# V's products in one run over all queries, the memory's normaliser applied to phi, and buffers kept as rings

## The chip, the cores and the metric

The kernel runs on one core of a Trainium2 chip. A core has TensorE (PE in the rows; its weight loads are PEld), VectorE (DVE), ScalarE (ACT), GpSimd (POOL) and SyncE, whose queue (SP) issues all the DMAs of this kernel. TensorE writes to PSUM, 8 banks of 512 fp32 columns in each of 128 partitions; the other data lie in SBUF. The metric is the device time of one execution in microseconds (us), less being better.

## The reference

Four batches, 8 heads, 576 queries of 64 elements: causal attention plus a linear "memory", mixed by a gate per head. The result is a 2304 x 512 matrix that goes through two feed-forward layers.

```
scores = scale * q @ k.T ; causal mask ; a = softmax(scores) ; local = a @ v
q_p  = where(q > 0, q, exp(q) - 1) + 1                    # phi(q)
mem_ret  = einsum('bhsd,bhde->bhse', q_p, M_prev)
mem_norm = einsum('bhsd,bhd->bhs', q_p, z_prev)[..., None] + 1e-06
g = 1 / (1 + exp(-beta))
x = g * mem_ret / mem_norm + (1 - g) * local              # to (2304, 512)
h = x @ w_in ;  x = (h * cos(h)) @ w_out                  # layer 1, inner width 2048
h = x @ w_in2 ; out = (h * tanh(softplus(h))) @ w_out2    # layer 2
```

## The kernel before, in words

Heads are worked on in pairs: 16 pairs (4 batches of 4), a pair being 128 partitions (two heads of 64). Queries come in 5 blocks of a pair, four of 128 and a last one of 64, in which the two heads stand side by side. The attention is a generator of 80 steps, one for each pair and block i, written as a pipeline: in step s, stage_c works on step s-4, then stage_b on s-2, then stage_a on s. prep of the next pair is called where i is 3.

- prep loads k, q, the memory's matrix, v and q once more, and makes phi (`ph`, transposed: 128 head elements x 576 queries) with two ScalarE instructions and one of VectorE (L217 to L219).
- stage_a: the scores on TensorE (L238, for the last block L251), masked minimum on VectorE (L240), exponential on ScalarE (L243), reciprocal of the sum (L263), and a scaling by it and by 1 - g on GpSimd (L265). Where i is 0 it calls memory first.
- memory multiplies each block of phi (as the weights) with the memory's matrix and the two normalisers beside it, 130 columns (L277), divides on VectorE (L280 to L282), and leaves `mo`, the memory's part by queries.
- stage_b transposes the scaled exponentials on TensorE (L297, L303); ScalarE or VectorE copies them to `aT` (L115, L117, the helper scaled).
- stage_c, for each block i: `mo` is transposed into a PSUM tile `o` by a product with the identity (L313), V's products add to it, for each of the i + 1 blocks of keys and each head one of 64 weight columns (L324); ScalarE makes the high part `xH` (L328) and VectorE the low part `xL` (L329), which are stored once per pair (L331, L332).

A product of two fp32 operands shows as two MATMUL records of one form in the trace, a transpose as one. The feed-forward layers split each operand in a high and a low fp32r part and use three products (L420 for h, L478 and L487 for y). Layer 1 is woven into the attention from batch 1 on (`next(m1)` in the main loop, paced by the steps of stage_c), and so is the conversion of its weights (L119 to L133, L163). What is left of layer 1, and all of layer 2, comes after the attention. A scheduler orders each engine's instructions when the program is built, from its own model of their times; on the chip each engine runs its list in that order, with semaphores between engines. A tile with `bufs=N` has at most N copies alive; which memory they have is found at that time too.

Of the kernel before, what the change touches and what calls it, by code (L numbers as in the profile page):

```python
# [20 lines left out]
BUFS = dict(  # L21
    mb=2, kd=4, qd=4, aD=4, vt=2, qt=1, ph=2, den=2, mo=4, xH=1, xL=3, sm=7, mn=2, at=8, aT=7, u=2, e=3, g=4, h=4, y=4, xb=3, yp=3, yh=2, yl=2, wst=2, S=6, T=8,
)
# [7 lines left out]
LAGC = 4  # L31
# [4 lines left out]
    wh="ap", aT="av", yl="p", ml="vp", y0="v", y1="a", aD="v",  # L36
# [7 lines left out]
def attention_moe_moe_kernel(  # L44
# [4 lines left out]
    qp: bass.AP,  # L49
    vn: bass.AP,  # L50
    mbd: bass.AP,
    beta: bass.AP,
# [51 lines left out]
    counts = {}  # L104

# [72 lines left out]
    def attention(ap, pools):  # L178
# [14 lines left out]
        def bank(tag, shape, name):  # L193
            turn[tag] += 1
            return pools[0].tile(shape, F32, tag=tag, name=name, bufs=BUFS[tag])

        pairs = [(b, p) for b in range(B) for p in range(NP)]
        prepd = {}

        def prep(b, p):  # L200
            st = {}

            kd = ap.tile([P, S], F32, tag="kd", name="kd", bufs=BUFS["kd"])
            nc.sync.dma_start(kd, kT[b, p])
            qd = ap.tile([P, S + D], F32, tag="qd", name="qd", bufs=BUFS["qd"])
            nc.sync.dma_start(qd, qT[b, p])
            st["q"], st["k"] = qd, kd
            mz = ap.tile([P, P + 2], F32, tag="mb", name="mz", bufs=BUFS["mb"])
            nc.sync.dma_start(mz, mbd[b, p])
            st["mz"] = mz  # L210
            vt = ap.tile([P, NQ, P], F32, tag="vt", name="vt", bufs=BUFS["vt"])
# [7 lines left out]
            nc.vector.scalar_tensor_tensor(ph, qt, 0.0, ph, ALU.max, ALU.add)  # L219
            st["ph"] = ph  # L220
            st["xH"] = ap.tile([P, S], F32R, tag="xH", name="xH", bufs=BUFS["xH"])
            st["xL"] = ap.tile([P, S], F32R, tag="xL", name="xL", bufs=BUFS["xL"])
            prepd[b, p] = st

        def stage_a(b, p, i):
# [6 lines left out]
            ats = [ap.tile([P, S], F32, tag="at", name="at", bufs=BUFS["at"]) for _ in range(2 if i < 4 else 1)]  # L232
# [35 lines left out]
        def memory(b, p):  # L268

            st = prepd[b, p]  # L270
            out = ap.tile([P, NQ, P], F32, tag="mo", name="mo", bufs=BUFS["mo"])
            for c0, c1 in ((0, 3), (3, NQ)):
                nb = c1 - c0
                mp = bank("T", [P, nb, P + 2], "mp")
                for c in range(c0, c1):
                    q0 = min(c * P, S - P)
                    nc.tensor.matmul(mp[:, c - c0], st["ph"][:, q0:q0 + P], st["mz"], start=True, stop=True)  # L277
                den = ap.tile([P, nb, 2], F32, tag="den", name="den", bufs=BUFS["den"])
                gg = igate[:, 2 * p:2 * p + 2].rearrange("q (o h) -> q o h", o=1).broadcast_to([P, nb, 2])
                nc.vector.scalar_tensor_tensor(den, mp[:, :, P:], 1e-6, gg, ALU.add, ALU.mult)  # L280
                nc.vector.reciprocal(den, den)  # L281
                nc.vector.tensor_tensor(  # L282
                    out[:, c0:c1].rearrange("q c (h d) -> q c h d", h=2),
                    mp[:, :, :P].rearrange("q c (h d) -> q c h d", h=2),
                    den.rearrange("q c (h o) -> q c h o", o=1).broadcast_to([P, nb, 2, D]), ALU.mult)
            st["mo"] = out

        def stage_b(b, p, i):
            st = prepd[b, p]
            n = P if i < 4 else D  # L290
            aTs = []
            for at in st["at", i]:
                tp = bank("T", [P, SM], "tp")
                aT = ap.tile([P, SM], F32, tag="aT", name="aT", bufs=BUFS["aT"])
                W = P * min(i + 1, 4)
                for c in range(0, W, P):
                    nc.tensor.transpose(tp[:, c:c + P], at[:, c:c + P], ident)  # L297
                scaled("aT", aT[:, :W], tp[:, :W], first=b == 0)
                aTs.append(aT)
            if i == 4:  # L300
                aD = ap.tile([P, 2, D], F32, tag="aD", name="aD", bufs=BUFS["aD"])
                tp = bank("T", [P, SM], "td")
                nc.tensor.transpose(tp[:D, :P], at[:, SM:], ident)  # L303
                scaled("aD", aD.rearrange("p a b -> p (a b)")[:D, :P], tp[:D, :P])
                aTs.append(aD)
            st["aT", i] = aTs

        def stage_c(b, p, i):
            st = prepd[b, p]
            n = P if i < 4 else D  # L310
            q0 = i * P
            o = bank("T", [P, P], "o")
            nc.tensor.matmul(o[:, :n], st["mo"][:, i], ident[:, P - n:], start=True, stop=False,  # L313
                             skip_group_check=True)
            for c in range(i + 1):
                kk = P if c < 4 else D
                for j in range(2):
                    if i < 4:
                        a = st["aT", i][j][:, c * P:(c + 1) * P]
                    elif c < 4:  # L320
                        a = st["aT", i][0][:, c * P + j * D:c * P + (j + 1) * D]
                    else:
                        a = st["aT", i][1][:D, j]
                    marks["pe"] = nc.tensor.matmul(  # L324
                        o[j * D:(j + 1) * D, :n], st["vt"][:kk, c, j * D:(j + 1) * D], a,
                        start=False, stop=c == i, skip_group_check=True).ins
            xH = st["xH"]
            nc.scalar.activation(xH[:, q0:q0 + n], o[:, :n], AF.Copy)  # L328
            nc.vector.tensor_tensor(st["xL"][:, q0:q0 + n], o[:, :n], xH[:, q0:q0 + n].bitcast(F32), ALU.subtract)  # L329
            if i == 4:  # L330
                nc.sync.dma_start(xsH[p, :, b * S:(b + 1) * S], xH.bitcast(F32))  # L331
                marks["sp"] = nc.sync.dma_start(xsL[p, :, b * S:(b + 1) * S], st["xL"].bitcast(F32)).ins  # L332
                del prepd[b, p]
# [333 lines left out]
```

## Time and profile before

| what | value |
|---|---|
| median of 3 runs | 1071.06 us (1069.19 to 1071.45) |
| profiled execution, first to last instruction | 1068.0 us |
| TensorE busy in it | 1042.6 us, 98% |
| VectorE, ScalarE, GpSimd busy | 490.7, 485.8, 391.6 us |

The profiled execution is given as its span; the times of the runs also hold what lies before the first and after the last instruction, some 3 us. "Busy" counts the time in which at least one record of an engine is open. Records of TensorE overlap, since products are pipelined, so the distance between starts tells more than the length of a record.

### The profile page before, as it was taken

To read this page: it belongs to the slowest core of one execution; us is meant where nothing else is said; L and a number is where in the kernel's file an instruction comes from. 1 tells how busy PE (TensorE), PEld (TensorE's weight loads), DVE (VectorE), ACT (ScalarE), POOL (GpSimd) and SP (SyncE) were. 2 spreads that over 40 slices of the span, in tenths; PEclk is the share of its full clock that TensorE was granted. 3 is DMA by queue.
4 is the path that set the end of the run, shared out by engine and by line. 5 is a ranking of instruction groups with operands and counts; after the bars stand their busy time and mean duration, and the time that the engine had idled before them with its cause. 6 is when DMAs were issued, how large, how long until landed. Compare 5 with 4: busy or idle time off the path is not lost.

```text
span 1068.0 us, 17139 instructions
## 1 busy us (share of the span) xinstructions
PE 1042.6 (98%) x6512; PEld 873.7 (82%) x6512; DVE 490.7 (46%) x1136; ACT 485.8 (45%) x1023; POOL 391.6 (37%) x425
## 2 busy tenths in 40 slices
PE   6997999999999999999999999999999999999998
PEld 4666688787878899998888889888888888888897
DVE  4588885445554558776766655665000000000000
ACT  6797875556564534344535454543322321222131
POOL 3377853323232334555555555654101010110100
PEclk8999999999999999999999999999999999999999
DMA  6366642323121275425345355630300300110010
GB/s 235 119 196 224 205 135 82 119 83 122 59 87 46 73 266 190 139 90 198 110 166 177 111 176 185 228 119 22 116 1 1 118 1 0 60 40 1 21 41 20
DMA packets 66369, 116.99 MB, mean 110 GB/s; under 512 B 5616, under 2 KB 25072, under 8 KB 66288
## 3 DMA queue, kind: packets, MB, share of 16 engines
q1 hardware_dynamic: 66288, 115.91, 32.2%
q8 instruction: 51, 0.84, 0.3%
q14 instruction: 30, 0.25, 0.1%
HBM read 87.58 MB, written 28.31 MB: 109 GB/s over the span
## 4 chain that ended last, share of the span: by engine, by line
PE 92%; ACT 2%; DVE 2%; DMA 2%; issue 1%; POOL 1%; SPq 0%; DVEq 0%; POOLq 0%; ACTq 0%
PE h L420 37%; PE y L478 20%; PE y L487 18%; PE o L324 5%; PE sp L238 4%; PE tp L297 4%; PE o L313 2%; PE mp L277 1%; PE sp L251 1%; DMA qt<-in_qp_dram 1%; DMA wst<-in_w1i_dram 1%; DVE at L240 1%; ACT at L243 1%; DMA vt<-in_vn_dram 1%; POOL at L265 0%
## 5 line engine op out<-in xcount | busy, mean ns | idle before, releaser
L420 PE MATMUL h<-xbH,w 128*128 128x256 f32 (+1 forms) x1536 | 393.0, 338 | 0.1
L420 PEld LDWEIGHTS h<-xbH,w 128*128 128x128 f32 x1536 | 266.9, 190 | 33.7 <-issue 1.0
L420 PE MATMUL h<-xbL,w 128*128 128x256 f32 (+1 forms) x768 | 258.0, 336 | 1.5 <-DMA xbL<-xsL 1.5
L478 PE MATMUL y<-g,w 128*128 128x256 f32 (+1 forms) x1344 | 221.5, 319 | 4.4 <-ACT aT L115 4.2
L478 PEld LDWEIGHTS y<-g,w 128*128 128x128 f32 x1344 | 193.1, 192 | 30.8 <-issue 9.4
L487 PE MATMUL y<-w,g 128*128 128x512 f32 x864 | 201.8, 389 | 0.0
L487 PEld LDWEIGHTS y<-w,g 128*128 128x128 f32 x864 | 161.9, 188 | 33.5
L392 DVE TENSOR_TENSOR g<-e,g 128x512 fp32r<-128x512 f32 x36 | 24.9, 691 | 297.1 <-ACT g L115 297.1
L420 PEld LDWEIGHTS h<-xbL,w 128*128 128x128 f32 x768 | 145.6, 190 | 16.9 <-DMA xbL<-xsL 1.7
L392 POOL TENSOR_TENSOR g<-e,g 128x512 fp32r<-128x512 f32 x36 | 47.8, 1328 | 286.5 <-ACT g L115 286.5
L265 POOL TENSOR_SCALAR at<-at,sm,omg 128x128 f32<-128x128 f32 (+2 forms) x144 | 102.7, 723 | 134.4 <-DVE sm L263 119.2
L384 ACT ACTIVATE e<-h 128x512 f32<-128x512 f32 x72 | 43.0, 597 | 232.5 <-PE h L420 231.0
L392 POOL TENSOR_TENSOR g<-u,g 128x512 fp32r<-128x512 f32 x72 | 102.0, 1436 | 121.5 <-ACT g L115 45.6
L367 ACT ACTIVATE u<-h 128x512 int32<-128x512 f32 x72 | 42.9, 595 | 111.9 <-PE h L420 104.2
L243 ACT ACTIVATE at<-at,mn 128x128 f32<-128x128 f32 (+3 forms) x128 | 70.9, 555 | 28.2 <-DVE mn L240 26.8
L129 DVE SCALAR_TENSOR_TENSOR wst<-wst 128x512 int32<-128x512 int32 x64 | 53.9, 843 | 37.7 <-POOL wst L119 31.3
L119 POOL TENSOR_SCALAR wst<-wst 128x512 f32<-128x512 f32 x64 | 46.4, 731 | 63.2 <-DMA wst<-in_w1i_dram 25.1
L297 PE MATMUL tp<-ident,at 128*128 128x128 f32 x384 | 63.9, 285 | 5.6 <-DVE den L281 2.2
L368 DVE SCALAR_TENSOR_TENSOR u<-u,h 128x512 f32<-128x512 int32 x72 | 49.0, 682 | 40.8 <-ACT u L367 40.5
L240 DVE CUSTOM_DVE_ANT_0 at<-sp,mask 128x128 f32<-128x128 f32 (+3 forms) x128 | 59.3, 482 | 17.6 <-PE sp L238 16.0
L133 DVE TENSOR_TENSOR wst<-wst 128x512 int32<-128x512 int32 x64 | 66.1, 1035 | 1.2
L324 PE MATMUL o<-aT,vt 128*64 128x128 f32 (+1 forms) x896 | 64.5, 272 | 1.7 <-ACT aT L115 1.5
(76 smaller groups left out, 1084.1 us busy)
## 6 DMA issues: line engine op xcount, KB each, us to landing
wst<-in_w1i_dram SPq DMA_DIRECT2D x16, 512.0 KB, 5.4
wst<-in_w1o_dram SPq DMA_DIRECT2D x16, 512.0 KB, 4.6
wst<-in_w2i_dram SPq DMA_DIRECT2D x16, 512.0 KB, 4.0
wst<-in_w2o_dram SPq DMA_DIRECT2D x16, 512.0 KB, 4.7
qd<-in_qT_dram SPq DMA_DIRECT2D x16, 320.0 KB, 3.4
vt<-in_vn_dram SPq DMA_DIRECT2D x16, 320.0 KB, 3.2
xbH<-xsH SPq DMA_DIRECT2D x20, 256.0 KB, 4.9
xbL<-xsL SPq DMA_DIRECT2D x20, 256.0 KB, 4.6
```

Source lines behind the costliest of these rows:

```text
L129: nc.vector.scalar_tensor_tensor(lo, hi, 3, lo, ALU.logical_shift_left, ALU.bitwise_or)
L133: nc.vector.tensor_tensor(dst, lo, hi, ALU.bitwise_xor)
L240: nc.vector.tensor_tensor_reduce(at[:, :N], sp[:, :N], mask[:, SM - q0:SM - q0 + N], SSC, 3.0e38, ALU.add, ALU.min, mn[:, j:j + 1])
L243: marks["act"] = nc.scalar.activation(at[:, :N], at[:, :N], AF.Exp, bias=mn[:, j:j + 1], scale=-1.0, accum_out=sm[:, j:j + 1]).ins
L265: turn_of("sc", b == 0).tensor_scalar(at[:, :N], at[:, :N], sm[:, j:j + 1], gates[j], ALU.mult, ALU.mult)
L297: nc.tensor.transpose(tp[:, c:c + P], at[:, c:c + P], ident)
L324: marks["pe"] = nc.tensor.matmul(o[j * D:(j + 1) * D, :n], st["vt"][:kk, c, j * D:(j + 1) * D], a, start=False, stop=c == i, skip_group_ch ...
L368: nc.vector.scalar_tensor_tensor(u, u.bitcast(I32), -TWO_PI, h, ALU.mult, ALU.add)
L392: turn_of(kind).tensor_tensor(gL, g, gH.bitcast(F32), ALU.subtract)
L420: nc.tensor.matmul(h[:, a * T:(a + 1) * T], w_[:, c, f0:f0 + P], x_[c], start=m == 0, stop=m == 3 * NC - 1)
L478: nc.tensor.matmul(y[e // per][:, cols], w_[:, f, es], g_, start=fst and m == 0 and e % per == 0, stop=lst and m == 2, skip_group_check=True)
L487: nc.tensor.matmul(y[t], g_[:, tsl], w_[:, f, :], start=fst and m == 0, stop=lst and m == 2, skip_group_check=True)
```

## The change

V's products of a pair wait until all its 5 blocks have been transposed, and run over all queries at once: for each block of keys and head, one product over all queries from that block on (512, 448, 320, 192 and 64 columns) into one bank `o`, and two small ones for the first 64 queries into another, `od`. The memory's normaliser is applied to phi, which is now laid out by queries: GpSimd multiplies phi with z, VectorE sums and takes the reciprocal, GpSimd scales phi; TensorE transposes the result (`pT`, copied by ScalarE), and the memory's matrix is multiplied once with all queries, straight into `od` and `o`. `mo`, its identity product and its division go. xH and xL are made in two instructions each per pair instead of five. Many tiles become slices of one larger tile used in turn (ring), kd and qd with 2 places instead of 4, xL with 2 instead of 3; `aT` is one tile for two pairs. On the host, q is laid out by queries (640 with padding) and z is handed over as rows, broadcast over partitions by a DMA of its own.

```diff
+    def ring(pool, tag, shape, dtype=F32):
+        if tag not in rings:
+            rings[tag] = [pool.tile([shape[0], BUFS[tag], *shape[1:]], dtype, name=tag), 0]
+        r = rings[tag]
+        r[1] += 1
+        return r[0][:, (r[1] - 1) % BUFS[tag]]
...
         def prep(b, p):
...
-            qt = ap.tile([P, S], F32, tag="qt", name="qt", bufs=BUFS["qt"])
-            nc.sync.dma_start(qt, qp[b, p])
-            ph = ap.tile([P, S], F32, tag="ph", name="ph", bufs=BUFS["ph"])
+            qt = ring(ap, "qt", [P, NQ, P], F32)
+            nc.sync.dma_start(qt, qn[b, p])
+            ph = ring(ap, "ph", [P, NQ, P], F32)
             nc.scalar.activation(ph, qt, AF.Relu, scale=-1.0)
             nc.scalar.activation(ph, ph, AF.Exp, scale=-1.0)
             nc.vector.scalar_tensor_tensor(ph, qt, 0.0, ph, ALU.max, ALU.add)
+            zb = ap.tile([P, P], F32, tag="zb", name="zb", bufs=BUFS["zb"])
+            nc.sync.dma_start(zb, zr[b, p].partition_broadcast(P))
+            nc.gpsimd.tensor_tensor(
+                qt, ph, zb.rearrange("q (o d) -> q o d", o=1).broadcast_to([P, NQ, P]), ALU.mult)
+            den = ap.tile([P, NQ, 2], F32, tag="den", name="den", bufs=BUFS["den"])
+            nc.vector.tensor_reduce(den, qt.rearrange("q c (h d) -> q c h d", h=2), AX.X, ALU.add)
...
+            nc.vector.scalar_tensor_tensor(den, den, 1e-6, gg, ALU.add, ALU.mult)
+            nc.vector.reciprocal(den, den)
+            nc.gpsimd.tensor_tensor(
+                ph.rearrange("q c (h d) -> q c h d", h=2), ph.rearrange("q c (h d) -> q c h d", h=2),
+                den.rearrange("q c (h o) -> q c h o", o=1).broadcast_to([P, NQ, 2, D]), ALU.mult)
...
         def memory(b, p):
...
+            pT = ring(ap, "pT", [P, S], F32)
+            for c0, c1 in ((0, 4), (4, NQ)):
+                w = min(c1 * P, S) - c0 * P
+                mp = bank("T", [P, SM], "mp")
                 for c in range(c0, c1):
+                    n = min(P, S - c * P)
+                    nc.tensor.transpose(mp[:, (c - c0) * P:(c - c0) * P + n], st["ph"][:n, c], ident[:n, :n])
+                scaled("pT", pT[:, c0 * P:c0 * P + w], mp[:, :w])
...
         def stage_b(b, p, i):
...
+                tc4 = tp.rearrange("k (c q) -> k c q", q=P)[:, :W]
+                if i < 4:
+                    scaled("aT", aT[j][:, :W, i * P:(i + 1) * P], tc4, first=b == 0)
+                else:
+                    for h in range(2):
+                        scaled("aT", aT[h][:, :, SM:], tc4[:, :, h * D:(h + 1) * D], first=b == 0)
...
+        def stage_c(b, p):
             st = prepd[b, p]
...
+            od = bank("T", [P, D], "od")
+            o = bank("T", [P, SM], "o")
+            for t, q0, q1 in ((od, 0, D), (o, D, S)):
+                nc.tensor.matmul(t, st["mz"], st["pT"][:, q0:q1], start=True, stop=False, skip_group_check=True)
+            for j in range(2):
+                nc.tensor.matmul(od[j * D:(j + 1) * D, :], vt[:D, 0, j * D:(j + 1) * D], aT[j][:D, 0, :D],
+                                 start=False, stop=True, skip_group_check=True)
+            for c in range(NQ):
+                q0 = max(c * P, D)
                 for j in range(2):
+                    kk = P if c < 4 else D
+                    a = aT[j][:, c, q0:] if c < 4 else aD[:D, j]
                     marks["pe"] = nc.tensor.matmul(
+                        o[j * D:(j + 1) * D, q0 - D:], vt[:kk, c, j * D:(j + 1) * D], a,
+                        start=False, stop=c == NQ - 1, skip_group_check=True).ins
+            xH, xL = st["xH"], st["xL"]
+            for t, q0, q1 in ((od, 0, D), (o, D, S)):
+                nc.scalar.activation(xH[:, q0:q1], t, AF.Copy)
+                nc.vector.tensor_tensor(xL[:, q0:q1], t, xH[:, q0:q1].bitcast(F32), ALU.subtract)
...
             if 0 <= s - LAGC < ns:
-                stage_c(*steps[s - LAGC])
+                if steps[s - LAGC][2] == NQ - 1:
+                    stage_c(*steps[s - LAGC][:2])
                 yield "c", s - LAGC
```

## Rows read from the trace of the kernel before

**Rows 1.** The page's first part: busy time of each engine, share, instructions.
```profile
PE 1042.6 (98%) x6512; PEld 873.7 (82%) x6512; DVE 490.7 (46%) x1136; ACT 485.8 (45%) x1023; POOL 391.6 (37%) x425
```

**Rows 2.** Stretches: length, busy us (instructions) by engine, clock, DMA share, GB/s.
```profile
16.00:75.00 59.00, 56.79 (x433) 38.44 (x435) 38.74 (x148) 47.96 (x150) 25.51 (x34) 0.94 0.48 156
75.00:150.00 75.00, 67.73 (x565) 51.49 (x565) 65.36 (x208) 56.03 (x151) 55.83 (x62) 0.98 0.59 193
150.00:380.00 230.00, 225.82 (x1921) 189.29 (x1921) 118.26 (x404) 129.95 (x328) 69.26 (x91) 0.99 0.26 83
380.00:1068.00 688.00, 684.09 (x3562) 589.55 (x3560) 261.57 (x346) 243.41 (x372) 233.28 (x202) 1.00 0.29 101
```

**Rows 3.** What idle PE waited for: us in total, times, longest.
```profile
PE y L478 <- ACT aT L115: 4.2, 3, 1.4
PE tp L297 <- DVE den L281: 2.2, 1, 2.2
PE o L313 <- DVE mo L282: 1.9, 1, 1.9
```

**Rows 4.** The chain that ended last, one pair's products: start us, us, what.
```profile
211.84 1.12 PE mp L277 x10
212.96 0.22 PE o L313 x2
213.19 0.81 PE o L324 x12
213.99 3.07 PE h L420 x24
...
218.65 1.02 PE o L324 x16
...
225.19 0.88 PE o L324 x20
...
229.13 0.44 PE tp L297 x4
229.57 1.06 PE sp L238 x4
...
232.97 0.37 PE o L324 x4
...
234.14 0.86 PE sp L251 x2
...
235.35 0.17 PE sd L251 x2
...
236.27 0.59 PE o L324 x8
```

**Rows 5.** The same chain just after the attention.
```profile
386.90 5.76 PE h L420 x48
```

**Rows 6.** Instructions of one form, 0 to 380 us: busy us, mean ns, idle before.
```profile
L392 POOL TENSOR_TENSOR g<-u,g 128x512 fp32r<-128x512 f32 x20 | 26.3, 1335 | 58.9 <-DVE g L117 27.6 <-ACT at L243 27.3 <-DVE sm L263 4.0
L329 DVE TENSOR_TENSOR xL<-o,xH 128x128 fp32r<-128x128 f32 x64 | 17.9, 285 | 11.9 <-ACT xH L328 11.4
L115 ACT ACTIVATE aT<-tp 128x512 f32<-128x512 f32 x30 | 17.6, 586 | 16.1 <-PE tp L297 16.0
L328 ACT ACTIVATE xH<-o 128x128 fp32r<-128x128 f32 x64 | 16.7, 266 | 11.9 <-PE o L324 10.4 <-PE h L420 1.0 <-DMA xsH<-xH 0.3
L375 DVE TENSOR_TENSOR u<-h,u 128x512 f32<-128x512 f32 x20 | 12.9, 686 | 5.5 <-ACT u L372 5.5
L282 DVE TENSOR_TENSOR mo<-mp,den 128x384 f32<-128x384 f32 x16 | 8.8, 552 | 0.0
L115 ACT ACTIVATE aT<-tp 128x256 f32<-128x256 f32 x20 | 7.2, 379 | 1.1 <-PE tp L297 1.1
```

**Rows 7.** The same for GpSimd's scaling, 16 to 75 us.
```profile
L265 POOL TENSOR_SCALAR at<-at,sm,omg 128x384 f32<-128x384 f32 x6 | 5.0, 835 | 6.8 <-DVE sm L263 6.8
```

**Rows 8.** The same, 75 to 150 us.
```profile
L265 POOL TENSOR_SCALAR at<-at,sm,omg 128x384 f32<-128x384 f32 x8 | 9.0, 1135 | 1.0 <-PE o L324 0.8 <-DVE sm L263 0.2
```

More of the change, by code (lines that the diff above doesn't have):

```diff
@@ L21 @@
 BUFS = dict(
-    mb=2, kd=4, qd=4, aD=4, vt=2, qt=1, ph=2, den=2, mo=4, xH=1, xL=3, sm=7, mn=2, at=8, aT=7, u=2, e=3, g=4, h=4, y=4, xb=3, yp=3, yh=2, yl=2, wst=2, S=6, T=8,
+    mb=2, kd=2, qd=2, aD=2, vt=2, qt=2, ph=2, zb=2, den=2, pT=2, xH=1, xL=2, sm=7, mn=2, at=8, u=2, e=3, g=4, h=4, y=4, xb=3, yp=3, yh=2, yl=2, wst=2, S=6, T=8,
 )
@@ L48, in attention_moe_moe_kernel @@
     kT: bass.AP,
-    qp: bass.AP,
+    qn: bass.AP,
     vn: bass.AP,
     mbd: bass.AP,
+    zr: bass.AP,
     beta: bass.AP,
@@ L104, in attention_moe_moe_kernel @@
     counts = {}
+    rings = {}
+    def ring(pool, tag, shape, dtype=F32):
[4 more added lines that the diff above has]
+        return r[0][:, (r[1] - 1) % BUFS[tag]]
     def turn_of(kind, first=False):
@@ L195, in bank @@
             return pools[0].tile(shape, F32, tag=tag, name=name, bufs=BUFS[tag])
+        aTr = ap.tile([P, 4, NQ - 1, S], F32, name="aTr")
+        turns = {}
         pairs = [(b, p) for b in range(B) for p in range(NP)]
@@ L231, in stage_a @@
             mn = ap.tile([P, 2], F32, tag="mn", name="mn", bufs=BUFS["mn"])
-            ats = [ap.tile([P, S], F32, tag="at", name="at", bufs=BUFS["at"]) for _ in range(2 if i < 4 else 1)]
+            ats = [ring(ap, "at", [P, S], F32) for _ in range(2 if i < 4 else 1)]
             if i < 4:
@@ L270, in memory @@
             st = prepd[b, p]
[L271 to L274, printed above, removed]
+            pT = ring(ap, "pT", [P, S], F32)
+            for c0, c1 in ((0, 4), (4, NQ)):
+                w = min(c1 * P, S) - c0 * P
+                mp = bank("T", [P, SM], "mp")
                 for c in range(c0, c1):
[L276 to L285, printed above, removed]
@@ L286, in memory @@
-            st["mo"] = out
+                    n = min(P, S - c * P)
+                    nc.tensor.transpose(mp[:, (c - c0) * P:(c - c0) * P + n], st["ph"][:n, c], ident[:n, :n])
+                scaled("pT", pT[:, c0 * P:c0 * P + w], mp[:, :w])
+            st["pT"] = pT
         def stage_b(b, p, i):
             st = prepd[b, p]
-            n = P if i < 4 else D
-            aTs = []
-            for at in st["at", i]:
-                tp = bank("T", [P, SM], "tp")
[L294 to L299, printed above, removed]
+            if i == 0:
+                r = turns["aT"] = (turns.get("aT", -1) + 1) % 2
+                st["aT"] = [aTr[:, 2 * r + h] for h in range(2)]
+                st["aD"] = ap.tile([P, 2, D], F32, tag="aD", name="aD", bufs=BUFS["aD"])
@@ new lines, in stage_b @@
+            aT = st["aT"]
+            W = min(i + 1, 4)
+            for j, at in enumerate(st["at", i]):
+                tp = bank("T", [P, SM], "tp")
+                for c in range(W):
+                    nc.tensor.transpose(tp[:, c * P:(c + 1) * P], at[:, c * P:(c + 1) * P], ident)
+                tc4 = tp.rearrange("k (c q) -> k c q", q=P)[:, :W]
[4 more added lines that the diff above has]
+                        scaled("aT", aT[h][:, :, SM:], tc4[:, :, h * D:(h + 1) * D], first=b == 0)
@@ L300, in stage_b @@
             if i == 4:
-                aD = ap.tile([P, 2, D], F32, tag="aD", name="aD", bufs=BUFS["aD"])
                 tp = bank("T", [P, SM], "td")
                 nc.tensor.transpose(tp[:D, :P], at[:, SM:], ident)
[L304 to L308, printed above, removed]
+                scaled("aD", st["aD"].rearrange("p a b -> p (a b)")[:D, :P], tp[:D, :P])
+        def stage_c(b, p):
@@ L309, in stage_c @@
             st = prepd[b, p]
[L310 to L316, printed above, removed]
-                for j in range(2):
[L318 to L323, printed above, removed]
-                    marks["pe"] = nc.tensor.matmul(
-                        o[j * D:(j + 1) * D, :n], st["vt"][:kk, c, j * D:(j + 1) * D], a,
-                        start=False, stop=c == i, skip_group_check=True).ins
@@ L327, in stage_c @@
[L327 to L333, printed above, removed]
+            aT, aD, vt = st["aT"], st["aD"], st["vt"]
@@ L335, in attention @@
+            xH, xL = st["xH"], st["xL"]
+            for t, q0, q1 in ((od, 0, D), (o, D, S)):
+                nc.scalar.activation(xH[:, q0:q1], t, AF.Copy)
+                nc.vector.tensor_tensor(xL[:, q0:q1], t, xH[:, q0:q1].bitcast(F32), ALU.subtract)
+            nc.sync.dma_start(xsH[p, :, b * S:(b + 1) * S], xH.bitcast(F32))
+            marks["sp"] = nc.sync.dma_start(xsL[p, :, b * S:(b + 1) * S], xL.bitcast(F32)).ins
+            del prepd[b, p]
         steps = [(b, p, i) for b, p in pairs for i in range(NQ)]
@@ L642 @@
         mbd[:, :, d, d] = m[:, j::2]
-        mbd[:, :, d, 2 * D + j] = zp[:, j::2]
     laid = [
-        ("qT", padded(q)), ("kT", pairs(k)), ("qp", pairs(q)), ("vn", rows(v)), ("mbd", mbd),
+        ("qT", padded(q)), ("kT", pairs(k)), ("qn", rows(q)), ("vn", rows(v)), ("mbd", mbd),
+        ("zr", inputs["z_prev"].reshape(B, NP, 2 * D)),
         ("beta", inputs["beta"]),
```

18 lines of the change are left out of this document (9 added, 9 removed).

## The prediction

> **What bounds the kernel now.** I read the page's first part, then the stretches, then what idle TensorE waited for, then the chain that ended last. TensorE is busy for 98% of the span and no other engine for half of it [rows 1]. Busy could still mean overlapping records, so the stretches come next: after 380 us, where only feed-forward work is left, TensorE idles 3.9 of 688 us; from 150 to 380 it idles 4.2 of 230, from 75 to 150 7.3 of 75, from 16 to 75 2.2 of 59 [rows 2]. So what the change takes off TensorE's list is worth its full length from 150 us on, if no new wait comes. In the two earlier stretches others are nearly as full: ScalarE 81% from 16 to 75, VectorE 87% and GpSimd 74% from 75 to 150. TensorE's idle time there is short waits; two of the larger ones, 2.2 and 1.9 us, ended with `den` and `mo` of the memory's division [rows 3]. The chain shows how dense the list is: in a stretch of one pair the memory's ten records end at 212.96, the identity product starts there, V's products follow at 213.19, and the next work of layer 1 at 213.99 [rows 4]. TensorE's order and length set the time.
>
> A number the page doesn't print can be read there. 24 records of h take 2.88 us where nothing else stands between them (half of [rows 5]) and 3.07 right behind V's products [rows 4]. The 0.19 is the price of going from V's 64-column weights back to the full array.
>
> **TensorE's list, per pair, before** [rows 4]: memory 1.12; five identity products at 0.22, 1.10; V's five runs 0.81 + 1.02 + 0.88 + 0.37 + 0.59 = 3.67; five returns at 0.19, 0.95. Sum 6.84 us.
>
> **After.** Five transposes at 0.11 (four take 0.44) are 0.55. The memory's matrix over 512 and 64 queries has the form of the last block's scores, 0.86 + 0.17 = 1.03. The four small records into `od` are 4 of 20 such in 0.88, 0.18. V's wide products: 16 records take 1.02 and 8 take 0.59, so 512 columns more cost 0.43, 0.84 ns each. The number of columns per pair stays: 2 x (512 + 448 + 320 + 192 + 64) = 3072 in `o`, 2.58 us, plus 0.16 that a run costs whatever its length (0.59 - 0.43), plus 0.32 because the first pass of a run has no other head beside it and is now 512 wide instead of 128 (0.43 against 0.11): 3.06. Returns: one out of the run, and three more for pieces of 64 rows (`od`, the last keys, the last transpose), 4 x 0.19 = 0.76. Sum 5.58: **1.26 us less per pair, 20.2 for 16**.
>
> No row shows a V product of 512 columns. Dear end: the rate of the scores, where two heads of 512 columns, 1024 in all, take 1.06 [rows 4]; 3072 columns are then 3.18 us instead of 2.58, and a pair saves 0.66, 10.6 in all. Cheap end: only the one return at the run's end costs, and a pair saves 1.83, 29.3 in all. I take 1.26, since V's runs differ from the scores in lying side by side by output columns, not by rows, and it is V's own rows that I extend.
>
> **The other engines, per pair** [rows 6]. ScalarE: xH was 4 x 0.266 and one of 64 columns (0.21, by 0.11 per 128 columns between copies of 128 and 256), 1.27; now 0.586 + 0.21. The two copies of pT are new, 0.80. The last block's aT copy becomes two of 256 columns, 2 x 0.379 for 0.586. Phi grows by 64 columns in two instructions, 0.14. Net +0.64. VectorE: the division goes, 0.552 and about 0.37 for 256 columns, with two tiny instructions on balance, some 0.3; xL goes from 4 x 0.285 to one of 0.686, 0.45 less; phi grows by 0.07. New is a reduction over 640 columns, not in the trace; from 0.686 for a two-input instruction of 512 it is at most 0.86, taken whole. Net -0.8. GpSimd: two products over 640 columns, by 1.335 for 512 they are 1.67 each, **3.34 us more per pair**. The cheap end is the one-input scaling of 384 columns, 0.835 [rows 7], 1.4 for 640.
>
> **What covers them.** The scaling of 384 columns comes twice in a pair: 6 and 8 of them mean 3 pairs in the stretch from 16 us and 4 in that from 75 [rows 7, 8]; with one before, 8 are left for 150 to 380, 28.8 us each.
> - 150 to 380: TensorE saves 8 x 1.26 = 10.1 of 230. ScalarE would be at 135, GpSimd at 96, VectorE at 112 of 220. Kept whole.
> - 16 to 75: saves 3.8. ScalarE goes to 47.96 + 1.9 = 49.9 of 55.2, 90%. It feeds TensorE through exponentials and copies in short turns, so I write off half, 1.9.
> - 75 to 150: saves 5.0. GpSimd goes to 55.83 + 13.4 = 69.2 of 70.0. It has no room, and I write off all 5.0.
> - The waits for `den` and `mo`, 4.1 us, lose their cause: `pT` is needed only by stage_c, eight steps behind memory instead of four. What is late next is the pair's exponentials; I count half, 2.0.
>
> The scaling took 0.835 us from 16 to 75 and 1.135 from 75 to 150 [rows 7, 8], while VectorE went from 66% to 87% busy [rows 2]. So GpSimd's new products may grow by 1.36 there, to 18.2 for four pairs, and GpSimd needs 74.0 of 75 us: the 5.0 stay written off, and nothing is left over.
> [...]
>
> **Queues.** SP issues one DMA more per pair (z's rows). The memory's matrix is now held until stage_c, so on SP its load waits for the stage_c of two pairs back, and v, q, z, weight pieces and x loads stand behind it. V's load had the same wait before; stage_c's end moves by some 4 us (4.3 of products in one run instead of 1.1 for the last block). Two steps of five, 11.5 us, cover it in the late pairs. If that cover goes, phi is late, but GpSimd alone queues behind it: its products stand ahead of scalings (rival 4). The rings and fewer kd and qd copies cost nothing: a place is taken again two pairs later, long after its last reader.
>
> **Sum.** 1071.06 - 20.2 + 1.9 + 5.0 - 2.0 = 1055.8. The profiled span is 1068.0, 3.1 under the median; the 3.1 lie outside the instructions and stay. **Forecast 1056 us**, its own range 1050 to 1061. A difference of 0.2% (2.1 us) is about what a measurement of this kernel can tell from none.
>
> **Rivals.**
> 1. Everything is kept, and both waits go: 1071.06 - 20.2 - 4.1 = 1047. For it: TensorE idles only 2.2 us from 16 to 75 though ScalarE is 81% full. Against: GpSimd's 69.2 of 70.0. 0.13.
> 2. Wide products run at the scores' rate, or the run is cut up by other work and the returns come back: 10.6 saved, of which 3.6 is written off as above, and 2.0 for the waits: 1062. Against: V's rows are flat at 0.84 ns. 0.18.
> 3. PSUM. `od` and `o` are held through a run of 4.3 us and their copies (0.586 + 0.686 for `o`, against 0.266 + 0.285 for a block now). If TensorE waits that 1.27 us for a bank once in each of the 12 pairs after 75 us, 15 us go: 1071, no gain. Against: idle TensorE waited for a copy three times, 1.4 us at the longest [rows 3]. 0.13.
> 4. Slower: GpSimd's products stand in its queue ahead of the scalings that TensorE's transposes wait for. Each pair where both are exposed costs 3.34. From 1056 it takes five pairs to reach 1073; in the 4 of the second stretch and 4 others it is 26.7 us: 1082. For it: GpSimd at 99% there. Against: after 150 us it has more than half free. 0.13.
>
> The forecast has 0.43. **Chances**: faster 0.43 + 0.13 + 0.18 and 0.03 of rival 3 = 0.77; same 0.07 of rival 3 and 0.02 of rival 4 = 0.09; slower 0.03 + 0.11 = 0.14. **Range** 1043 to 1071: below lies the cheap end of the wide products (1071.06 - 29.3 = 1042), above it rival 4 and what of rival 3 is dearer, together under 0.2.
>
> **What would show it.** The four records of two heads' 512 columns take 0.86 us if V's price is right, 1.06 if rival 2 is. The stretch after the attention must be as now, and layer 1's work woven in must end some 15 us earlier. From 75 to 150 GpSimd should be the fullest engine; if TensorE idles there for `at`, rival 4 is at work; if it idles for copies of `o`, rival 3. The forecast is wrong if the scheduler's new list has waits that no product explains, since that list is made anew as a whole.

## The result, and the profile after

The change made the kernel slower: 1079.4 us (1077.8 to 1080.5, 4 runs) against 1071.3 (1069.2 to 1072.0), ratio 1.0076, interval 1.0060 to 1.0092. The forecast was 1056. The profiled execution took 1076.7 us, 8.7 more than before.

The page's first part, after:

```profile
PE 1041.4 (97%) x5760; PEld 839.1 (78%) x5760; DVE 501.5 (47%) x1046; ACT 494.0 (46%) x1017; POOL 438.1 (41%) x457
```

TensorE has 752 records fewer than in [rows 1] and is busy as long: what it no longer has to do, it spends at a lower rate or waiting. The stretches, with the columns of [rows 2], say where:

```profile
16.00:75.00 59.00, 52.52 (x269) 29.94 (x270) 40.49 (x134) 47.28 (x148) 41.89 (x52) 0.90 0.50 159
75.00:150.00 75.00, 68.99 (x381) 42.51 (x382) 62.48 (x176) 55.49 (x150) 59.66 (x62) 0.93 0.56 171
150.00:380.00 230.00, 224.76 (x1517) 170.62 (x1517) 125.44 (x364) 138.16 (x326) 94.52 (x111) 0.99 0.32 100
380.00:500.00 120.00, 115.20 (x867) 110.27 (x864) 90.89 (x124) 47.77 (x67) 59.78 (x55) 0.99 0.50 165
380.00:1076.70 696.70, 688.32 (x3574) 592.27 (x3570) 265.59 (x347) 245.19 (x373) 235.28 (x202) 1.00 0.30 99
```

TensorE idles 6.5 us from 16 to 75 (2.2 before), at a clock of 0.90 (0.94). From 380 us on it idles 8.4 us (3.9 before), and more than half of that lies between 380 and 500, where before it was busy 119.75 of 120:

```profile
380.00:500.00 120.00, 119.75 (x893) 114.83 (x892) 86.18 (x128) 50.26 (x72) 60.41 (x59) 1.00 0.57 196
```

The last product of the attention starts at 381.9 after and at 379.2 before, and none of the code behind it was changed.

What idle TensorE waited for, as in [rows 3]:

```profile
PE sp L263 <- DMA kd<-in_kT_dram: 6.7, 2, 4.7
PE tp L317 <- DVE mn L265: 4.9, 3, 3.3
PE y L499 <- DVE yp L127: 3.7, 1, 3.7
PE o L335 <- DVE mn L265: 3.0, 1, 3.0
PE h L441 <- DMA xbH<-xsH: 3.0, 2, 2.5
PE mp L302 <- POOL ph L242: 2.2, 1, 2.2
PE tp L317 <- POOL at L290: 0.2, 1, 0.2
```

The waits for `den` and `mo` are gone, as they should be; others have come (4.7 us of the first line are the kernel's start, where it was 4.5 before). Of GpSimd, the scalings (`at`) held TensorE up for 0.2 us, its product on phi once for 2.2.

A pair's products in the chain that ended last, for comparison with [rows 4] (start us, us, what):

```profile
219.07 0.64 PE mp L302 x5
...
228.17 0.17 PE od L335 x2
228.34 0.26 PE od L337 x2
228.59 1.06 PE o L335 x2
229.65 0.26 PE od L337 x2
229.90 2.89 PE o L344 x20
```

They sum to 5.28 us, where the same terms were forecast at 4.82: transposes 0.64 (0.55), the memory's matrix 1.23 (1.03), the two pieces of `od` 0.52 (0.18), V's run 2.89 (3.06). These distances hold the array's returns within the run, at `od` and at the last keys, which the forecast counted apart, at 0.19 each; with them it had 5.20. So the list did get shorter, and the question is where that went. To add it up over the span I give each record its distance between starts at full clock, by its form, and 0.095 us for each change of the array's form (two make the 0.19 of the prediction). By this estimate TensorE's list is 996.3 us before and 981.0 after, 15.3 less (20.2 forecast), and all time above it between TensorE's first and last product, waits and lower clock, is 63 us before and 87 after. Below, "excess" is this time above the list. It grew by 1.5 us before 16 us, by 4.5 from 16 to 75, 4.3 from 75 to 150, 6.1 from 150 to 380, and 7.5 from 380 to 500.

### The profile page after: what moved, and what is told of

Read it like the earlier page. It is cut to its first block, busy times and chain, and to the rows that moved or that the text cites. A ratio compares the mean times of both kernels' runs of the same rounds, so it can differ in the third digit from the quotient of the medians.

```text
span 1076.7 us, 15612 instructions
## 1 busy us (share of the span) xinstructions
PE 1041.4 (97%) x5760; PEld 839.1 (78%) x5760; DVE 501.5 (47%) x1046; ACT 494.0 (46%) x1017; POOL 438.1 (41%) x457
## 4 chain that ended last, share of the span: by engine, by line
PE 80%; DVE 6%; DMA 5%; POOL 3%; ACT 3%; issue 2%; POOLq 0%; DVEq 0%; ACTq 0%
PE h L441 33%; PE y L508 18%; PE y L499 14%; PE o L344 4%; PE tp L317 4%; PE sp L263 4%; DMA wst<-in_w1o_dram 2%; DMA wst<-in_w1i_dram 2%; POOL at L290 1%; PE o L335 1%; DVE wst L139 1%; DVE wst L140 1%; DVE wst L143 1%; PE mp L302 1%; DVE u L396 1%
## 5 line engine op out<-in xcount | busy, mean ns | idle before, releaser
L138 ACT ACTIVATE wst<-wst,c_seven 128x512 int32<-128x512 uint32 x64 | 49.2, 770 | 64.4 <-DMA wst<-in_w1o_dram 17.9
L263 PE MATMUL sp<-kd,qd 64*128 64x256 f32 (+3 forms) x256 | 69.1, 498 | 9.1 <-DMA kd<-in_kT_dram 6.7
L139 DVE SCALAR_TENSOR_TENSOR wst<-wst 128x512 int32<-128x512 int32 x64 | 55.6, 869 | 38.8 <-ACT wst L138 19.7
```

What stands on the lines that cost most here:

```text
L138: nc.scalar.activation(lo, lo.bitcast(U32), AF.Relu, scale=-(2.0 ** -29), bias=c_seven)
L139: nc.vector.scalar_tensor_tensor(lo, hi, 3, lo, ALU.logical_shift_left, ALU.bitwise_or)
L263: nc.tensor.matmul(sp[:, :N], st["q"][rows, q0:q0 + P], st["k"][rows, :N], start=True, stop=True)
```

## Experiments

Twelve kernels ran. They are told in the order of the argument; the first four were sent with three theories in mind: that GpSimd's products on phi cost the time (P), that V's products in one run do (W), or that no part does and the scheduler's new list fell badly (O). A time is the median of several runs, a trace that of one run, which need not be near the median. "Places" is in how many different addresses of SBUF the staging tile of the weight conversion (`wst`, 4 KB of a partition) lies in turn during the conversion of the half of layer 1's weights that follows the attention, read off the program as built. Its `bufs` is 2 in each kernel that keeps it a pool tile, so this count follows from how the tiles were packed.

| kernel | places | median us | ratio to before, interval | TensorE busy of the 120 us from 380 |
|---|---|---|---|---|
| before | 4 | 1071.3 | | 119.75 |
| changed | 2 | 1079.4 | 1.0076 [1.0060, 1.0092] | 115.20 |
| rings alone | 4 | 1066.1 | 0.9952 [0.9929, 0.9974] | 120.00 |
| rings, staging held to 2 | 2 | 1074.7 | 1.0037 [1.0022, 1.0052] | 117.37 |
| wide run alone, with rings | 2 | 1078.2 | 1.0072 [1.0048, 1.0096] | 112.76 |
| the same, packed | 4 | 1068.7 | 0.9972 [0.9955, 0.9989] | 118.95 |
| changed, packed | 4 | 1068.9 | 0.9979 [0.9963, 0.9995] | 119.97 |
| the same without GpSimd's products | 4 | 1061.2 | 0.9903 [0.9873, 0.9932] | 120.00 |
| normaliser alone, with rings | 4 | 1077.4 | 1.0054 [1.0034, 1.0074] | 120.00 |
| changed, products on VectorE | 2 | 1077.4 | 1.0057 [1.0039, 1.0076] | 114.98 |
| packed, products issued earlier | 4 | 1069.9 | 0.9988 [0.9973, 1.0003] | 119.94 |
| packed, normaliser by TensorE | 4 | 1094.9 | 1.0220 [1.0182, 1.0259] | 119.36 |
| packed, first batch divides | 4 | 1079.6 | 1.0072 [1.0052, 1.0093] | 119.97 |
| the same, products on VectorE | 4 | 1070.3 | 0.9994 [0.9977, 1.0010] | 119.97 |

**Rings alone.** The kernel before with the changed kernel's rings and counts of places.

```diff
-            kd = ap.tile([P, S], F32, tag="kd", name="kd", bufs=BUFS["kd"])
+            kd = ring(ap, "kd", [P, S], F32)
...
-            st["xL"] = ap.tile([P, S], F32R, tag="xL", name="xL", bufs=BUFS["xL"])
+            st["xL"] = ring(ap, "xL", [P, S], F32R)
```

> The kernel before with its tiles kept as rings and with the changed kernel's counts (kd and qd 2 places for 4, xL 2 for 3, qt 2 for 1). Theories P and W: 1069 to 1073, as before. If the rings or the fewer places are at fault: 1075 or more. Theory O allows a few us either way.

1066.1 us: this part by itself makes the kernel faster, by 0.5%, outside of what P and W expected. No trace shows where the 5 us come from: the profiled run took 1069.1, and its span is 0.7 us shorter than that of the kernel before.

**The wide run alone.** The rings, and V's products in one run; the memory is still divided on VectorE and comes in through the identity (qt has one place, mo two).

```diff
-            for t, q0, q1 in ((od, 0, D), (o, D, S)):
-                nc.tensor.matmul(t, st["mz"], st["pT"][:, q0:q1], start=True, stop=False, skip_group_check=True)
+            mo = st["mo"]
+            nc.tensor.matmul(od, mo[:, 0], ident[:, :D], start=True, stop=False, skip_group_check=True)
...
```

> The wide run of V's products and the rings, with the memory's division by queries and its identity products as in the kernel before. Theory P (the two products on GpSimd, 2.8 us per pair, hold up VectorE and the scalings in the first 180 us; the wide run itself is good): TensorE's list is shorter than before by some 0.7 us per pair, the early waits are like those of before, 1060 to 1064 us. Theory W (the one run per pair is at fault: it stands as a block of 5 us in TensorE's list and delays the stores of x): 1075 or more, with waits for x's load as in the changed kernel. Theory O (no part is at fault, the list made anew fell badly): anything from 1060 to 1080.

1078.2 us, though GpSimd has no products here. P alone falls. Against the rings alone 12 us are lost, and TensorE is busy only 112.76 of the 120 us from 380: the late loss comes with the wide run.

**The normaliser alone.** The changed kernel with V's five runs per pair, as before.

```diff
-                if steps[s - LAGC][2] == NQ - 1:
-                    stage_c(*steps[s - LAGC][:2])
+                stage_c(*steps[s - LAGC])
```

> The normaliser applied to phi and the rings, with V's products in five runs per pair as before (the memory's matrix is multiplied with each block of pT instead of the identity). Theory P: TensorE's list is some 8 us shorter than before and yet the time is 1075 to 1085, with TensorE's early waits on VectorE's masked minimum. Theory W: 1060 to 1068, the shorter list is kept. Theory O: anything.

1077.4 us, in P's range, but the profiled run was the lowest of the ten, 1070.75 (the next took 1075.2). In that trace there is no late loss at all (120.00 of 120), and the excess is early: by the estimate 9.3 us above that of the rings alone in the first 150. So the late loss is the wide run's and not the normaliser's; where the other 6.6 us up to the median go, no trace shows.

**The products on VectorE.**

```diff
-            nc.gpsimd.tensor_tensor(
+            nc.vector.tensor_tensor(
                 qt, ph, zb.rearrange("q (o d) -> q o d", o=1).broadcast_to([P, NQ, P]), ALU.mult)
...
-            nc.gpsimd.tensor_tensor(
+            nc.vector.tensor_tensor(
                 ph.rearrange("q c (h d) -> q c h d", h=2), ph.rearrange("q c (h d) -> q c h d", h=2),
```

> The changed kernel with the two products of the normaliser on VectorE (some 0.9 us each for 640 columns) instead of GpSimd. Theory P in the form that GpSimd's queue holds up the scalings, and that the two engines block each other: faster than the changed kernel, 1065 to 1073. If VectorE's own fullness from 75 to 150 us (62 of 75 us) is the limit: slower, 1080 to 1088. Theory W: as the changed kernel, 1077 to 1082.

1077.4 us, W's reading; the interval overlaps with the changed kernel's, and the late loss stays (114.98).

**What is late after the attention.** A conversion step by step, in the changed kernel's order of time (start us, us, engine, line, out<-in, idle before and what ended it):

```profile
459.44 0.37 SPq L135 DMA_DIRECT2D wst<-in_w1i_dram  x1
463.32 0.78 ACT L138 ACTIVATE wst<-wst,c_seven 128x512 int32<-128x512 uint32 x1 [2.16 <-DMA wst<-in_w1i_dram]
464.18 0.69 DVE L139 SCALAR_TENSOR_TENSOR wst<-wst 128x512 int32<-128x512 int32 x1 [2.19 <-ACT wst L138]
465.25 1.28 DVE L396 TENSOR_TENSOR u<-h,u 128x512 f32<-128x512 f32 x2
468.44 0.68 DVE L127 COPY yp<-y 128x512 f32<-128x512 f32 x1
469.17 3.17 PE L499 MATMUL y<-g,w 128*128 128x256 f32 x15 [3.66 <-DVE yp L127]
```

The load of a weight piece is issued at 459.44; ScalarE gets it at 463.32, having stood 2.16 us for it, and VectorE, whose list runs in order, stands 2.19 us before its own step. Behind that step in VectorE's list are u, g and the copy that empties y's bank, and TensorE stands 3.66 us for that copy. Why is the load so late? What SP's queue stood for at that load, 380 to 480 us, in the changed kernel and before:

```profile
SPq L135 <- DVE w L173: 21.4, 7, 5.3
SPq L135 <- DVE wst L143: 20.5, 6, 6.3
SPq L135 <- POOL w L173: 16.5, 7, 3.5
```

```profile
SPq L125 <- DVE wst L133: 8.5, 3, 4.4
SPq L125 <- POOL w L163: 7.6, 3, 2.6
SPq L125 <- DVE w L163: 4.7, 1, 4.7
```

The load waits for steps of an earlier piece's conversion (`w` is the last), 58 us in 20 waits against 21 in 7: it waits for its place. In the changed kernel the loads of the 5th to 7th piece go out at 406.8, 413.6 and 417.1, to the tenth when the conversion of the 3rd to 5th ends; before, the 4th to 6th had all gone out by 399.1, ahead of the end of the 3rd (404.6). This gave a third theory (S): `aTr`, 36.9 KB of each partition held through the attention, leaves the staging two places instead of four.

**Four places with the wide run, two without.** For the first, `aTr` is packed: a later block of keys has fewer queries, so a stride of 448 columns holds its 576, which frees 4.6 KB of each partition; qt and xL have one place instead of two, another 4.9 KB.

```diff
-        aTr = ap.tile([P, 4, NQ - 1, S], F32, name="aTr")
+        CS = S - P
+        RS = 3 * CS + S
+        aTr = ap.tile([P, 4 * RS + 3 * P], F32, name="aTr")
...
-                st["aT"] = [aTr[:, 2 * r + h] for h in range(2)]
+                st["aT"] = [(2 * r + h) * RS for h in range(2)]
...
-                    a = aT[j][:, c, q0:] if c < 4 else aD[:D, j]
+                    a = aTr[:, aT[j] + c * CS + q0:aT[j] + c * CS + S] if c < 4 else aD[:D, j]
```

> The changed kernel with the transposed probabilities packed (a stride of 448 columns for a block's run over 576 queries, since a later block begins 128 queries later) and one place fewer for qt and for xL, so that the staging of the weight conversion lies in four places of SBUF as in the kernel before, not in two. Same work on every engine. If the late stall (440 to 470 us, TensorE 112 busy of the 120 us from 380 to 500) comes from having only two pieces in flight: 7 to 9 us come back, 1070 to 1072 us, and TensorE is busy 119 or more of 380 to 500. If it comes from the long run of V's products itself (the conversion's instructions queue behind other work on VectorE, ScalarE or GpSimd): 1079 us and the same stall. The waits before 230 us stay in either case.

For the second, the rings alone with two places of staging:

```diff
-        st = wk.tile([P, SM, 2], I32, tag="wst", name="wst", bufs=BUFS["wst"])
+        st = ring(wk, "wst", [P, SM, 2], I32)
```

> The kernel before with the rings, which was 1066 us, with the staging of the weight conversion held in a ring of two places, not four. If two places make the late stall: 7 to 9 us more, 1073 to 1075 us, with TensorE busy 111 to 113 of the 120 us from 380 to 500 although V's products run as in the kernel before. If they don't: 1066 us and no stall there.

And the wide run alone, packed:

```diff
-        aTr = ap.tile([P, 4, NQ - 1, S], F32, name="aTr")
+        aTr = ap.tile([P, 4 * RS + 3 * P], F32, name="aTr")
```

> The wide run of V's products alone (the memory divided and brought in by identity products as before), which was 1078 us with two staging places, with the transposed probabilities packed so that staging has four. If the staging was the whole of its loss: 11 us come back, 1067 us, and against the kernel before with rings (1066) the wide run is then worth nothing or up to its 7 us of saved drains. If the wide run costs by itself: 1074 to 1078 us.

1068.9 for the changed kernel packed, 10.5 us back; 1074.7 for the rings held to two places, 8.5 us lost; 1068.7 for the wide run packed, 9.5 back. SP's waits for the load, 380 to 480 us, in the changed kernel packed, and behind them in the rings held to two places:

```profile
SPq L135 <- POOL w L173: 5.5, 3, 2.6
SPq L135 <- DVE w L173: 4.5, 2, 2.5
SPq L135 <- DVE wst L143: 3.0, 2, 1.8
```

```profile
SPq L135 <- DVE wst L143: 37.9, 7, 8.3
SPq L135 <- POOL w L173: 15.2, 7, 2.6
SPq L135 <- DVE w L173: 14.5, 4, 5.6
```

That is 13 us in 7 waits, and 68 in 18. The stretch from 380 to 500 of the first and of the second:

```profile
380.00:500.00 120.00, 119.97 (x881) 114.51 (x881) 97.06 (x129) 49.97 (x71) 69.21 (x61) 1.00 0.50 169
```

```profile
380.00:500.00 120.00, 117.37 (x896) 112.21 (x897) 81.21 (x125) 47.79 (x68) 58.86 (x56) 1.00 0.50 166
```

The wait follows the number of places, not V's run: S is shown in both directions. The rings held to two places have 2.6 us of idle time there, less than the 7 to 9 expected, but idle time isn't all of it. Counted in columns of the feed-forward products, which are the same in all kernels, the stretch from 380 to 500 does 249 thousand in them and 259 with four places, 5.0 us of work at the latter's rate; 238 in the changed kernel and 259 in it packed, 10.0 us; 235 and 255 in the wide run alone, 9.6 us. W falls too as the reason of the late loss: with its places back, the wide run by itself is 2.6 us above the rings alone (0.9972 against 0.9952, intervals overlapping), which this measurement can't tell from nothing. The packed version, whose trace is of the lowest of its ten runs (1065.7), also lost the excess of 150 to 230 us (7.2 for 15.2), though the waits before 230 were expected to stay; whether by the places, or since its second batch was stored at another time, isn't told apart.

**What GpSimd's products cost.** The packed version without them: phi isn't normalised, and `den` comes from phi itself.

```diff
-            nc.gpsimd.tensor_tensor(
-                qt, ph, zb.rearrange("q (o d) -> q o d", o=1).broadcast_to([P, NQ, P]), ALU.mult)
...
-            nc.vector.tensor_reduce(den, qt.rearrange("q c (h d) -> q c h d", h=2), AX.X, ALU.add)
+            nc.vector.tensor_reduce(den, ph.rearrange("q c (h d) -> q c h d", h=2), AX.X, ALU.add)
...
-            nc.gpsimd.tensor_tensor(
-                ph.rearrange("q c (h d) -> q c h d", h=2), ph.rearrange("q c (h d) -> q c h d", h=2),
-                den.rearrange("q c (h o) -> q c h o", o=1).broadcast_to([P, NQ, 2, D]), ALU.mult)
```

> As the kernel with four staging places, with the normaliser's two products on GpSimd left out (the output of the memory is then not normalised, and den is reduced from phi itself). If those products hold up the early stretch (GpSimd full to 69 of 70 us in 75 to 150, and VectorE's two-input operation drawn out from 0.77 to 1.62 us beside one): excess over the model of TensorE's list in 16 to 150 us falls from 42 to 33 us, and the time by 6 to 10 us against the kernel with four places. If the wait is for the products' place in the order alone or for something else: within 3 us of it.

1061.2 us: without the products it is 7.6 less, as the first reading had it. In the two traces, 4.6 us apart, TensorE's idle time from 16 to 150 us falls by 4.6, from 16.1 to 11.5. The list was made anew here as well, so how much of the 7.6 is the products' own isn't shown. How a product gets in the way can be seen at 71 us in the changed kernel:

```profile
71.75 1.42 POOL L242 TENSOR_TENSOR ph<-ph,den 128x640 f32<-128x640 f32 x1
72.09 1.62 DVE L143 TENSOR_TENSOR wst<-wst 128x512 int32<-128x512 int32 x1
74.30 0.41 DVE L265 CUSTOM_DVE_ANT_0 at<-sp,mask 128x256 f32<-128x256 f32 x1
74.87 1.51 PE L317 MATMUL tp<-ident,at 128*128 128x128 f32 x6 [3.34 <-DVE mn L265]
```

VectorE's conversion step, 0.69 us in the median with nothing of GpSimd beside it, takes 1.62; the masked minimum behind it comes late, and TensorE stands 3.34 us. The product accounts for some 0.9 of these; the rest is what else stands ahead of the minimum in VectorE's list, four steps of the conversion from 70.4 to 74.4 us.

**Is it the products' place in the order?** The packed version with the next pair prepared at the pair's second step, not its fourth (and one place for z's rows). In it a place of v's ring is refilled for the next pair before the pair that held it is through with it, so a part of the output comes from another pair's v; the work is the same.

```diff
-PREP = 3
+PREP = 1
```

> The 1069 us version (four staging places, phi normalised in every batch) with the next pair's preparation, the two products among it, issued at the pair's second step and not its fourth, some 8 us earlier in the first batch. If the normaliser costs because mp's transposes wait for a product that comes too late: 1062 to 1065 us. If it costs by the time that it takes of GpSimd and VectorE, wherever it stands: 1067 to 1071.

1069.9 us: no, the second reading. That they cost by the time that they take of GpSimd and VectorE is what is left of the two readings; which of the two engines it is, isn't shown.

**The normaliser without GpSimd.** z stands as a block matrix, a product on TensorE spreads phi.z over a head's 64 columns, ScalarE scales, VectorE takes the reciprocal of all 576 columns and multiplies.

```diff
-                    nc.tensor.transpose(mp[:, (c - c0) * P:(c - c0) * P + n], st["ph"][:n, c], ident[:n, :n])
+                nc.tensor.matmul(mp[:, :w], st["zb"], st["ph"][:, c0:c1], start=True, stop=True)
...
+            nc.vector.reciprocal(pT, pT)
+            nc.vector.tensor_tensor(pT, st["ph"], pT, ALU.mult)
```

> Four staging places as in the 1069 us version, but the normaliser is worked out by TensorE: phi lies by head elements, a product with a block matrix of z spreads phi.z over a head's 64 columns, ScalarE scales it by the gate, VectorE takes the reciprocal of 576 columns and one product. GpSimd has none of it and there are no transposes of phi. If what the normaliser costs is GpSimd's hold in the first batch: 1061 to 1064 us, near the version without products (1061). If the first batch wants VectorE as much (65 of 75 us busy from 75 to 150), two operations of 576 columns there cost as much or more: 1069 us or above.

1094.9 us. The second reading's side, and far beyond it: VectorE and ScalarE have no room for this either (TensorE's transposes stood 5.4 us for copies of aT and 3.8 for pT, both on ScalarE, and the scores 4.9 for VectorE's masked minimum).

**Division in the first batch, normaliser in the others.**

```diff
+            st["divide"] = b == 0
...
+            if st["divide"]:
+                nc.tensor.matmul(od, mo[:, 0], ident[:, :D], start=True, stop=False, skip_group_check=True)
...
```

> Four staging places and the wide run everywhere; in the first batch (to about 150 us, where VectorE, ScalarE and GpSimd are full and TensorE waits) the memory is divided after its product as in the kernel before, and in the other three batches phi is normalised as in the changed kernel. If the normaliser on phi costs in the first batch alone, the 12 later pairs keep its 0.66 us each of TensorE's list: the wide version with division was 1069 us, less 8 is 1061. If GpSimd's products also cost where TensorE is the bound: 1066 to 1069.

1079.6 us for this mixed version, 19 over what was expected. Excess was 15.4 us from 150 to 230 (7.8 with the wide run alone). There a product of GpSimd again lies over a step of VectorE:

```profile
166.98 1.65 POOL L246 TENSOR_TENSOR qt<-ph,zb 128x640 f32<-128x640 f32 x1 [1.89 <-DVE ph L239]
167.15 2.02 DVE L140 SCALAR_TENSOR_TENSOR wst<-wst 128x512 int32<-128x512 int32 x1
169.09 0.54 DVE L276 CUSTOM_DVE_ANT_0 at<-sp,mask 128x384 f32<-128x384 f32 x1
169.70 1.22 PE L375 MATMUL o<-mo,mz 128*128 128x512 f32 x1 [2.15 <-DVE mn L276]
```

So the same with the products on VectorE (and one place for phi, with which staging keeps four):

```diff
-            nc.gpsimd.tensor_tensor(
+            nc.vector.tensor_tensor(
```

> As the version whose first batch divides the memory after its product and whose other three normalise phi (1080 us, four staging places), with the two products of phi on VectorE, not GpSimd, and one place for phi. In that version one GpSimd product (167.0 to 168.6 us) had drawn VectorE's conversion step beside it out to 2.02 us, TensorE then stood 2.1 us and ran at the lower clock to 175 us. If that collision is what its second batch lost: the excess of 150 to 230 us falls from 15 to 7 or 8 us and the time to 1070 to 1073. If the loss comes with two schemes of memory in one order of work, or from any product between the batches: 1077 to 1081 us and the excess stays.

1070.3 us, in the range of the first reading, but not for its reason: the excess of 150 to 230 stayed at 14.5 us, with TensorE waiting for a copy of aT by VectorE (1.7 us) and for weights and x. What fell is the excess of the first 150 us, 52.2 to 46.5, where the two kernels have the same instructions until the second batch is prepared, and differ in phi's place. The scheduler orders the whole list anew for each kernel, and by this pair some 6 us can come and go with that; theory O stays open for every difference of that size here. Why the mixed version is slow stays open too.

## Why the prediction was wrong

**The step that failed is the sentence on places**: "The rings and fewer kd and qd copies cost nothing: a place is taken again two pairs later, long after its last reader." That weighed each tile against its own readers, and not the room that all of them leave to others; for the one large tile of transposed probabilities it has no term at all. `aTr`, 36.9 KB, is held through the attention; the staging of the next weights lost two of its four places, and that costs 10.5 us after the attention, where "must be as now" stood in the text as a check and no rival was built on it. The rings by themselves leave four places, and cost nothing indeed: they gave 5, for a reason that stays open.

**The sum, in parts that ran.** From 1071.3: the rings -5.1; the wide run, the shorter list and the division gone, as far as the products don't count, -4.9; GpSimd's products +7.6; two places of staging +10.5. That is 1079.4. Each difference has an interval of about 3 us, and the parts are taken in this order: another would give them other shares (the normaliser on V's five runs lost 11 us, on the wide run, against division, nothing). Only the last part has a wait that was taken away and brought back; the first three are of the size that a new list can make by itself.

**TensorE's list**: right in kind, 15.3 us by the estimate above for 20.2. V's wide products run at V's rate, as taken: 20 records in 2.89 us, 3.06 forecast, and the four of two heads' 512 columns in 0.91, where 0.86 was to speak for V's rate and 1.06 for the scores'. So rival 2 falls by its first condition. By its second, that other work cuts up the run, it came true in part: in 8 of the 16 pairs the scheduler put transposes or scores behind the run's first two records. The four then take 1.34 us at full clock, which makes 3.4 for the 8, the larger part of the 4.9 that the list lacks.

**The write-offs**: 6.9 us before 150 were too few, and "150 to 380: kept whole" failed too: layer 1's work woven in was to end some 15 us earlier, and at 380 us the same 13.8% of the feed-forward columns are done as before. Even without the products, the list shorter by 15 us gave 4.9. With the wide run packed, the clock from 16 to 75 us was 0.81, against 0.94 with the rings alone, and the excess there 18.1 for 13.2 (from 75 to 150 the clock was the higher one, 0.98 for 0.93). In the first batch, with only attention to do, a shorter list seems to turn into waiting; this is read from the stretches, and no run tests it. From 75 to 150 GpSimd was not the fullest engine: 59.7 us for the 69.2 forecast, with VectorE at 62.5; from 16 to 75 it had 16.4 us more than before.

**GpSimd's products**: 1.57 and 1.27 us each, forecast 1.67; the price is not in their length alone. Of rival 4's 0.13, 0.03 has no row or run behind it: none shows VectorE stopped through the whole of each product. What the runs showed in its place: VectorE's step of 72.09 us ended 0.54 us after the product beside it, and the mixed version's of 167.15 us as well; alone, such a step takes 0.69. In all, the steps drawn out beside the products on phi took some 11 us more of VectorE in the changed kernel's trace than they take alone, all before 170 us. That they make the 7.6 fits, and isn't shown: with the products on VectorE itself the changed kernel took 1077.4 for 1079.4.

**The rivals**: the waits for `den` and `mo` went, as forecast. Rival 3 falls, no wait for copies of `o` is in the list. Rival 4 named the slower side, 1082, and GpSimd, but by scalings that come late (0.2 us in all); that its number lies near the measured one is luck, since 10.5 us of the loss lie after the attention.

## What to carry to other kernels

A tile that is made one large piece and held longer takes room from tiles that no line of the change touches: see which tiles lie in how many places before and after, and which load then waits for the end of an earlier use. Work taken off the fullest engine counts in the stretches where that engine's list sets the time; in the others look first at who feeds it. And a change that is worth a few us has to be weighed against what a new list does by itself, here some 6. The best version found that does the whole work is the kernel before with the rings alone, 1066.1 us, 0.5% below before.

## What the runs showed of the hardware

In the changed kernel's trace some of VectorE's instructions that began beside a GpSimd product of two SBUF operands ended only after it, and others took as long as alone. Counted are those that had 0.3 us or more of the product left. The conversion's steps with two inputs in SBUF ended 0.55 us after it, each of them (L139, 9 of them; L143, 25; L173, 8); alone they take 0.69. Phi's step over 640 columns, also with two inputs in SBUF, ended 0.68 after it (L231, 4) and takes 0.82 alone. Two kinds with a single input, both over 512 columns from SBUF to SBUF and 0.43 and 0.42 us long alone, ended 0.28 after it (L140, 23; the cast of g, 5). Those that read PSUM stayed as they were (medians, alone and beside a product): the masked minimum over 512 columns 0.69 and 0.68, xL 0.69 and 0.69, copies of 256 columns to aT 0.42 and 0.41; and so did the reciprocal of the sums in SBUF, 0.16 and 0.16. An instruction of 10 columns (L240), 0.16 alone, took 1.60 at 19.21 us and ended 0.03 after a product that had begun 0.32 us later than it. What sets these kinds apart, no run tests.

In three places of the changed kernel a lower clock followed a wait of TensorE. It stood 3.34 us until 74.87, and the granted clock was 0.50 from 75 to 78 us and 0.99 from 78 to 80; 2.52 until 176.19, and 0.50 from 178 to 180, 1.00 from 181 to 190; 3.66 until 469.17, and 0.50 from 471 to 474, 1.00 from 474 to 500. The mixed version's TensorE was busy 6.1 of the 8 us from 160 to 168, then stood the 2.15 us above until 169.70. The whole stretch:

```profile
160.00:180.00 20.00, 16.41 (x87) 9.39 (x84) 10.92 (x24) 9.42 (x22) 11.82 (x15) 0.83 0.28 89
```

It holds 3.6 us of idle time, and a mean clock of 0.83 over 20 us is by estimate another 3.4 us of full clock. In the changed kernel packed, with TensorE busy throughout, the clock there is 1.00, and 143 records are done (of another mix) instead of 87. The mixed version with its products on VectorE has 0.83 there as well, so the fall doesn't hang on GpSimd's product alone.
